# Interleaved runs of columns in the MLP's matmuls: another order for the moving operand and the PSUM output

## The chip, the cores and the metric

The kernel runs on one core of a Trainium2 chip. The metric is the device time of one execution in microseconds (us); smaller is better. The kernel before took 358.94 us (median of 2 runs, 358.88 and 359.0).

## The reference

The program adds three terms: the input `x` (2048 tokens of 448 channels), a gated long convolution of branch A, and an MLP on the layer-normalised input. Cut to what matters:

```python
x = A_q                                    # (1, 2048, 448), float32
xn = _layernorm(x, axis=-1)
# branch A: short causal convolution of k (4 taps), times v, long causal
# convolution with ssm_k through a 4096-point FFT, plus kv * ssm_D, times xn
# branch B:
h = xn @ w1 + b1                           # w1: 448 x 1792
sp = log1p(exp(-|h|)) + max(h, 0)
act = h * tanh(sp)                         # Mish
out = x + A(xn, k, v, ...) + act @ w2      # w2: 1792 x 448
```

The change touches branch B alone. What it computes stays the same.

## The kernel before, in words

**Branch A** is an FFT written as matmuls in plain float32. Its three steps on TensorE are a first transform (`f1_mm`, line 148), an inner transform with its inverse (`f2_mm`, line 237, and `i1_mm`, line 276) and a last transform (`i2_mm`, line 330). They work on parts of the 128 x 128 array: the call at line 237 makes eight matmuls of 448 columns, each on its own block of 64 rows and 32 columns of the array, and the trace holds two records for each of them. VectorE does the four taps, the products and the folds between these steps, GpSimd one tap of each group. Intermediate results go through DRAM.

**Branch B** splits each float32 operand into a high part, rounded to the type `fp32r`, and a low part, and adds three products (high x high, high x low, low x high). The 2048 tokens form 8 chunks of 256 tokens (`CH`), the 1792 inner channels 14 tiles of 128, taken two at a time: a *pair* is one chunk `c` with two inner tiles, `p` from 0 to 6. There are 8 x 7 = 56 pairs, worked in order. For each pair:

- `g1_mm` (line 494) makes 2 x 11 = 22 matmuls at line 514. The stationary operand is a 128 x 128 block of `w1h` or `w1l`, the moving one 256 contiguous columns of `XH` or `XL`, and the output 256 contiguous columns of a PSUM bank. The two inner tiles `n` share a bank, one in each half.
- `mish` (line 517) has ScalarE apply Mish to each 256 columns of PSUM (line 522) into the tile `a`, then cast `a` to its high part `ach` (line 86); VectorE subtracts for the low part `acl` (line 87).
- `g2_mm` (line 536) makes 2 x 2 x 3 = 12 matmuls at lines 546 to 548. The stationary operand is a 128 x 128 block of `ach` or `acl`, the moving one 448 contiguous columns of `w2h` or `w2l`, the output 448 contiguous columns of a PSUM bank, which sums over the seven pairs of the chunk. VectorE then adds that bank to `x` (line 553).

**The order of the work** is written out by hand: a plan by half-slots says when each step of branch A, each load and each split is issued, and `mlp_slot` puts the second layer of a pair two pairs after its first (`G2_LAG`). Each engine takes its instructions in that order. In the octave stage of branch A (slots 66 to 89) the PSUM banks are shared: `mish` of some pairs reads a bank that a transform matmul writes next.

Of the kernel before, what the change touches and what calls it, by code (L numbers as in the profile page):

```python
# [9 lines left out]
AF = mybir.ActivationFunctionType  # L10
# [6 lines left out]
NF = F // 128  # L17
# [21 lines left out]
EVAC_SOON = 2,  # L39
WARM_N = (448, 448, 448)  # L40
FILL_N = (224, 112, 96)


@with_exitstack
def tile_kernel(ctx: ExitStack, tc, q, qT, k, v, sk, hT, sD, w10, w1, w2, c_fib, c_g, c_gi, c_i2, out):
    nc = tc.nc
# [25 lines left out]
    b1t = cp.tile([128, NF], F32, name="b1t")  # L72
# [9 lines left out]
    w2h = wp.tile([128, NF, D], F32R, name="w2h")  # L82
    w2l = wp.tile([128, NF, D], F32R, name="w2l")

    def split(h, l, raw):
        nc.scalar.copy(h, raw)  # L86
        V.tensor_sub(l, raw, h)  # L87
# [4 lines left out]
    def bank(n):  # L92
        return duo[n // 2][:, n % 2]

    def pg():
        return g1p[0].tile([128, 512], F32, name="pg1")
# [9 lines left out]
    def dv(n=1):  # L106
        for _ in range(n):
            if drip:
                drip.pop(0)()
# [257 lines left out]
    def w1_hi(p, a=0, b=256):  # L367
        nc.scalar.copy(w1h[:, :, 256 * p + a:256 * p + b], w1_raw(p, a, b))

    def w1_lo(p, a=0, b=256):  # L370
        fs, rw = slice(256 * p + a, 256 * p + b), w1_raw(p, a, b)
        V.tensor_sub(w1l[:, :, fs], rw[:, 0:3], w1h[:, 0:3, fs])  # L372
        V.tensor_sub(w1h[64:128, 3, fs], rw[64:128, 3], w1h[64:128, 3, fs])
# [120 lines left out]
    def g1_mm(i):  # L494
        c, p = pairs[i]
        XH, XL = XS[c]
        pt = [(bank(GB[i]) if i in GB else pg()).rearrange("p (a b) -> p a b", a=2) for _ in range(2 if i == 0 else 1)]
        ps = [pt[n % len(pt)][:, n] for n in range(2)]
        mm = [[], []]
        for n in range(2):  # L500
            f = 2 * p + n
            fs = slice(128 * f, 128 * f + 128)
            hh, hl, lh = ([(w[:, kt, fs], x[:, kt]) for kt in range(3)] for w, x in ((w1h, XH), (w1h, XL), (w1l, XH)))
            th, tl = ((w1h[:, 3, fs], x[:, 3]) for x in (XH, XL))
            mm[n] = [(n, *m) for m in hh + lh + [th] + hl + [tl]]

            if 0 < i < NP:
                mm[n] = [(n, *m) for m in hh + hl + lh + [th, tl]]
        if i == 0:
            seq = mm[0][:7] + mm[1][:3] + mm[0][7:] + mm[1][7:10] + mm[1][3:7] + mm[1][10:]  # L510
        else:
            seq = mm[0] + mm[1]
        for n_, (n, l, r) in enumerate(seq):
            nc.tensor.matmul(ps[n], l, r, start=all(m[0] != n for m in seq[:n_]), stop=all(m[0] != n for m in seq[n_ + 1:]))  # L514
        P1[i] = ps

    def mish(i):
        p = pairs[i][1]
        ps = P1.pop(i)
        a = mp.tile([128, 2, CH], F32, name="a", bufs=2)  # L520
        for n in range(2):
            nc.scalar.activation(a[:, n], ps[n], AF.Mish, bias=b1t[:, 2 * p + n:2 * p + n + 1])  # L522
            if i == n == 0:
                w1_hi(2)
        if i == 0:
            w1_lo(2)
        ah = mp.tile([128, 2, CH], F32R, name="ach", bufs=3)
        al = mp.tile([128, 2, CH], F32R, name="acl", bufs=3)
        AHL[i] = ah, al
        if 2 * i + 1 in hv:  # L530
            held.append(lambda: split(ah, al, a))
        else:
            split(ah, al, a)
            dv()

    def g2_mm(i, jjs=(0, 1)):
        c, p = pairs[i]
        ah, al = AHL[i]
        for n in range(2):
            f = 2 * p + n  # L540
            for jj in jjs:
                if f == 0:
                    P2[c, jj] = g2p.tile([128, 512], F32, name="pg2")
                ps = P2[c, jj][:, :D]
                cs = slice(128 * jj, 128 * jj + 128)
                nc.tensor.matmul(ps, ah[:, n, cs], w2h[:, f], start=f == 0, stop=False)  # L546
                nc.tensor.matmul(ps, ah[:, n, cs], w2l[:, f], start=False, stop=False)  # L547
                nc.tensor.matmul(ps, al[:, n, cs], w2h[:, f], start=False, stop=f == NF - 1)  # L548

    def g2_evac(c, jjs=(0, 1)):  # L550
        x = Q[c]
# [9 lines left out]
    def mlp_slot(s):  # L561
# [3 lines left out]
        if half == 0:  # L565
            if i < n:
                c, p = pairs[i]
                if c + 1 < NT:
                    if p == 0:
                        ln_load(c + 1)  # L570
                    if p == (3 if c in (0, 2) else 2):
                        ln_stats(c + 1)
                    if c == 0:
                        dv(len(drip))
                    if p == NP - 1:
                        ln_T(c + 1, 1)
                g1_mm(i)
        else:
            if i < n:
                c, p = pairs[i]  # L580
                if p == NP - 2 and c + 1 < NT:
                    ln_T(c + 1, 0)
                if s not in hv:
                    mish(i)
            if 0 <= j < n - 1:
                g2_mm(j)
                if pairs[j][1] == NP - 1 and pairs[j][0] in EVAC_SOON:
                    g2_evac(pairs[j][0])
            elif j == n - 1:
                for jj in range(2):  # L590
                    g2_mm(j, (jj,))
                    g2_evac(pairs[j][0], (jj,))
# [79 lines left out]
    for c in range(NT, NCHUNK):  # L672
        at_ = NT_HOW.get(c, NT_AT)
        b = 2 * NP * (c - 1) + (1 if c < 5 else 0)
# [42 lines left out]
    ps = [g2p.tile([128, 512], F32, name="pg2") for _ in range(2)]  # L717
# [3 lines left out]
    def filler(n, w=wz):  # L721
        k = w.shape[1]
        nc.tensor.matmul(fill[0:k, 0:n], w, wz[:, 0:1].to_broadcast([128, n]), start=True, stop=True)

    filler(FILL_N[0], ve[:, 0:1])
    filler(FILL_N[1], ve[:, 1:2])
    for jj in range(2):
# [3 lines left out]
        if jj == 0:  # L731
            filler(FILL_N[2])
            w1_hi(0, 0, 128)
# [13 lines left out]
    for s in range(nslots):  # L747
        j = s // 2 - G2_LAG - 1
        if s % 2 == 0 and j >= 0 and pairs[j][1] == NP - 1 and pairs[j][0] not in EVAC_SOON:
            g2_evac(pairs[j][0])  # L750
        if s in hv:
            mish(s // 2)
        for fn, args in plan.pop(s, ()):
            fn(*args)
        mlp_slot(s)
        fns = plan2.pop(s, ())
        for fn, args in fns:
            if fn is i1_out:
                fn(*args)
        for fn, args in fns:  # L760
            if fn is not i1_out:
                fn(*args)
# [69 lines left out]
```

## Time and profile before

| what | value |
|---|---|
| median of the runs | 358.94 us (358.88, 359.0) |
| profiled execution: span from first to last instruction | 357.0 us |
| TensorE (PE) busy | 351.0 us, 98% of the span, 3092 matmul records |
| weight loads (PEld) busy | 289.5 us, 81% |
| VectorE (DVE) busy | 270.6 us, 76% |
| ScalarE (ACT) busy | 156.6 us, 44% |
| GpSimd (POOL) busy | 70.3 us, 20% |
| mean granted TensorE clock | 0.998 |

The profile gives for the profiled execution its span alone, not a time of its own measured as the runs are. The median of the runs is 1.9 us above that span; this is what lies around the first and the last instruction.

How to read it: a row of a group names the line, the engine, the operation, output<-inputs, the shapes and the count, then busy us, the mean ns of one instruction and the idle time before them. A matmul's duration covers its way through the array, and the next one starts before it ends. What a matmul costs in a stream is therefore the distance from its start to the next start, which the timeline and the chain of waits show, not its duration. All matmul operands read `f32` there, `fp32r` too.

### The profile page before, as it was taken

The numbers are of one execution on the slowest core, as the hardware profiler recorded it, in microseconds if no ns is written. First come the engines' busy times: TensorE is split into PE (matmuls) and PEld (weight loads), VectorE is DVE, ScalarE is ACT, GpSimd is POOL, SyncE is SP. The second block draws the span as 40 slices with busy tenths as digits, with TensorE's granted clock in tenths as the row PEclk, the third lists the DMA queues.
The fourth block names the chain that finished last, engine by engine and source line by source line (L and its number), as shares of the span: only waits on it lengthen the run. The fifth ranks groups of instructions, "written<-read, shape, count | busy, mean of one in ns | idle before, by whom it ended". The sixth has DMA issues, their size and how long they took to land.

```text
span 357.0 us, 7437 instructions
## 1 busy us (share of the span) xinstructions
PE 351.0 (98%) x3092; PEld 289.5 (81%) x3092; DVE 270.6 (76%) x375; ACT 156.6 (44%) x267; POOL 70.3 (20%) x78
## 2 busy tenths in 40 slices
PE   8999999999999999999999999999999999999995
PEld 2988888888888989888988757666775699979794
DVE  5989748999999999999437756756963933788941
ACT  4966552344243343343233454445445443354470
POOL 2037002822220240212000031011031116040030
PEclk9999999999999999999999999999999999999999
DMA  7998976949768637665869569999896387989086
GB/s 260 344 364 307 411 287 175 340 123 263 198 171 313 164 107 168 223 162 118 245 201 355 201 165 292 248 278 312 276 273 121 77 234 272 409 319 274 19 116 141
DMA packets 30691, 83.27 MB, mean 233 GB/s; under 512 B 3137, under 2 KB 15810, under 8 KB 30658
## 3 DMA queue, kind: packets, MB, share of 16 engines
q1 hardware_dynamic: 21842, 47.82, 39.4%
q0 software_dynamic: 4928, 22.95, 22.9%
q10 hardware_dynamic: 3888, 12.03, 12.8%
q8 instruction: 24, 0.39, 0.4%
q14 instruction: 9, 0.07, 0.1%
HBM read 54.34 MB, written 28.45 MB: 232 GB/s over the span
## 4 chain that ended last, share of the span: by engine, by line
PE 52%; issue 8%; DVE 6%; POOL 2%; DMA 1%
PE pq L514 7%; PE pg L546 7%; PE pg L548 7%; PE pg L547 6%; PE pp L514 5%; PE pr L514 4%; PE pp L237 3%; PE pr L237 3%; PE pp L276 2%; PE pg L514 2%; DVE x L201 2%; POOL x L184 2%; PE pq L237 2%; DMA xn<-in_qT_dram 1%; PE pr L276 1%
## 5 line engine op out<-in xcount | busy, mean ns | idle before, releaser
L546 PE MATMUL pg<-w2h,ach 128*128 128x448 f32 x224 | 82.5, 368 | 0.0
L548 PE MATMUL pg<-w2h,acl 128*128 128x448 f32 x224 | 81.4, 363 | 0.0
L547 PE MATMUL pg<-w2l,ach 128*128 128x448 f32 x224 | 81.2, 362 | 0.0
L87 DVE TENSOR_TENSOR acl<-a,ach 128x512 fp32r<-128x512 f32 x56 | 38.9, 695 | 31.7 <-ACT ach L86 31.5
L522 ACT ACTIVATE a<-pg,b1t 128x256 f32<-128x256 f32 x66 | 27.8, 472 | 65.4 <-PE pg L514 43.3
L514 PE MATMUL pg<-XH,w1h 128*128 128x256 f32 x264 | 52.6, 283 | 0.0
L546 PEld LDWEIGHTS pg<-w2h,ach 128*128 128x128 f32 x224 | 41.9, 187 | 11.5 <-issue 7.2
L514 PEld LDWEIGHTS pg<-XH,w1h 128*128 128x128 f32 x264 | 41.4, 188 | 6.9 <-issue 5.6
L547 PEld LDWEIGHTS pg<-w2l,ach 128*128 128x128 f32 x224 | 42.1, 188 | 2.4
L548 PEld LDWEIGHTS pg<-w2h,acl 128*128 128x128 f32 x224 | 42.1, 188 | 2.4
L514 PE MATMUL pg<-XL,w1h 128*128 128x256 f32 x264 | 42.9, 277 | 0.0
L158 DVE TENSOR_TENSOR st<-pq,st 128x896 f32<-128x896 f32 x32 | 34.8, 1089 | 4.8 <-ACT st L154 4.3
L514 PEld LDWEIGHTS pg<-XL,w1h 128*128 128x128 f32 x264 | 35.9, 188 | 0.0
L86 ACT CAST ach<-a 128x512 fp32r<-128x512 f32 x56 | 34.8, 622 | 1.7
L514 PE MATMUL pg<-XH,w1l 128*128 128x256 f32 x198 | 33.6, 278 | 0.0
L184 POOL TENSOR_TENSOR x<-kr,skb 128x896 f32<-128x896 f32 x8 | 17.0, 2123 | 70.9 <-PE pr L148 26.2
L514 PEld LDWEIGHTS pg<-XH,w1l 128*128 128x128 f32 x198 | 27.6, 188 | 0.2 <-DVE w1l L372 0.2
L201 DVE TENSOR_TENSOR x<-x 128x896 f32<-128x896 f32 x24 | 26.2, 1091 | 1.5 <-POOL x L184 0.8
L522 ACT ACTIVATE a<-pq,b1t 128x256 f32<-128x256 f32 x20 | 8.4, 471 | 31.8 <-PE pq L514 31.8
L287 POOL DMA_DIRECT2D E<-qe x14 | 8.7, 628 | 63.1 <-ACT qe L284 63.1
L154 ACT COPY st<-pr 128x896 f32<-128x896 f32 x16 | 14.5, 908 | 14.2 <-PE pr L148 12.3
L417 POOL TENSOR_TENSOR mv<-ve,mhalf 128x2 f32<-128x2 f32 x5 | 5.0, 1007 | 72.0 <-DVE ve L414 72.0
(138 smaller groups left out, 605.7 us busy)
## 6 DMA issues: line engine op xcount, KB each, us to landing
Dkv<-st ACTq DMA_DIRECT2D x16, 448.0 KB, 5.3
ah<-Dh SPq DMA_DIRECT2D x8, 896.0 KB, 7.5
av<-Dkv SPq DMA_DIRECT2D x8, 896.0 KB, 8.6
e<-E POOLq DMA_DIRECT2D x8, 896.0 KB, 7.2
E<-qe POOLq DMA_DIRECT2D x14, 448.0 KB, 5.9
kr<-in_k_dram SPq DMA_DIRECT2D x10, 448.0 KB, 6.8
Dh<-st ACTq DMA_DIRECT2D x10, 448.0 KB, 6.2
x<-in_hT_dram SPq DMA_DIRECT2D x8, 448.0 KB, 6.0
```

What stands on the lines that cost most here:

```text
L86: nc.scalar.copy(h, raw)
L87: V.tensor_sub(l, raw, h)
L154: nc.scalar.copy(st[:, 1], o)
L158: f(st[:, n], e, st[:, 1])
L184: nc.gpsimd.tensor_mul(o, KR[g - u // 2], skb[:, u:u + 1].to_broadcast([128, 2, D]))
L201: V.tensor_add(KV[g], KV[g], o)
L237: nc.tensor.matmul(p[32 * t:32 * t + 32, r, :D], g[rs, t, c], a[rs, t], start=True, stop=True, tile_position=(64 * r, 32 * t))
L514: nc.tensor.matmul(ps[n], l, r, start=all(m[0] != n for m in seq[:n_]), stop=all(m[0] != n for m in seq[n_ + 1:]))
L522: nc.scalar.activation(a[:, n], ps[n], AF.Mish, bias=b1t[:, 2 * p + n:2 * p + n + 1])
L546: nc.tensor.matmul(ps, ah[:, n, cs], w2h[:, f], start=f == 0, stop=False)
L547: nc.tensor.matmul(ps, ah[:, n, cs], w2l[:, f], start=False, stop=False)
L548: nc.tensor.matmul(ps, al[:, n, cs], w2h[:, f], start=False, stop=f == NF - 1)
```

## The change

Two tables give run lengths for some pair numbers `p`; `p = 0` is in neither and stays as it was. A helper turns 2·b·c contiguous columns into b groups of two runs of c columns: run 0 of the first half, run 0 of the second half, run 1 of the first half, and so on. The columns are the same, in another order.

- **Second layer** (`RUNS`): for p = 1 to 6 the moving operand and the PSUM output are both taken in runs of 16, 8, 32, 2, 4 and 112 columns, the two halves being 224 columns apart. Both are permuted alike, so each column lands where it did before.
- **First layer** (`RUNS1`, run length of the read and of the write; 0 is contiguous; the halves are 128 columns apart): p = 1 reads and writes in runs of 16, p = 5 in runs of 2. There too each column lands where it did. p = 2 reads in runs of 16 and p = 3 in runs of 2, and both write contiguously, so PSUM holds the columns in another order; `mish` restores it by writing `a` in such runs. p = 4 reads contiguously and writes in runs of 16; `mish` reads PSUM in such runs.

Counts, from the loops: 8 chunks x 5 pairs x 22 = 880 of the 1232 first-layer matmuls, 8 x 6 x 12 = 576 of the 672 second-layer matmuls, and 8 x 3 x 2 = 48 of the 112 activations. Every instruction is still one instruction with the same number of columns, and every engine has the same instructions in the same order.

```diff
+RUNS = {1: 16, 2: 8, 3: 32, 4: 2, 5: 4, 6: 112}
+RUNS1 = {1: (16, 16), 2: (16, 0), 3: (2, 0), 4: (0, 16), 5: (2, 2)}
...
+        ri, ro = RUNS1.get(p, (0, 0))
         for n_, (n, l, r) in enumerate(seq):
-            nc.tensor.matmul(ps[n], l, r, start=all(m[0] != n for m in seq[:n_]), stop=all(m[0] != n for m in seq[n_ + 1:]))
+            nc.tensor.matmul(runs(ps[n], ro), l, runs(r, ri), start=all(m[0] != n for m in seq[:n_]), stop=all(m[0] != n for m in seq[n_ + 1:]))
         P1[i] = ps
+
+    def runs(t, c):
+        return t.rearrange("p (a b c) -> p b a c", a=2, c=c) if c else t
 
     def mish(i):
...
-            nc.scalar.activation(a[:, n], ps[n], AF.Mish, bias=b1t[:, 2 * p + n:2 * p + n + 1])
+            ri, ro = RUNS1.get(p, (0, 0))
+            o = runs(a[:, n], ri) if ro != ri else a[:, n]
+            nc.scalar.activation(o, runs(ps[n], ro) if ro != ri else ps[n], AF.Mish, bias=b1t[:, 2 * p + n:2 * p + n + 1])
...
     def g2_mm(i, jjs=(0, 1)):
         c, p = pairs[i]
+        r = (lambda t: t.rearrange("p (a b c) -> p b a c", a=2, c=RUNS[p])) if p in RUNS else lambda t: t
...
-                nc.tensor.matmul(ps, ah[:, n, cs], w2h[:, f], start=f == 0, stop=False)
-                nc.tensor.matmul(ps, ah[:, n, cs], w2l[:, f], start=False, stop=False)
-                nc.tensor.matmul(ps, al[:, n, cs], w2h[:, f], start=False, stop=f == NF - 1)
+                nc.tensor.matmul(r(ps), ah[:, n, cs], r(w2h[:, f]), start=f == 0, stop=False)
+                nc.tensor.matmul(r(ps), ah[:, n, cs], r(w2l[:, f]), start=False, stop=False)
+                nc.tensor.matmul(r(ps), al[:, n, cs], r(w2h[:, f]), start=False, stop=f == NF - 1)
```

## The prediction

> **What bounds the kernel now.** I read the page's totals first, then its chain of work, then the list of what the matmuls waited for, and last the distances between matmul starts. The page:
>
> ```profile
> span 357.0 us, 7437 instructions
> PE 351.0 (98%) x3092; PEld 289.5 (81%) x3092; DVE 270.6 (76%) x375; ACT 156.6 (44%) x267; POOL 70.3 (20%) x78
> ...
> PEclk9999999999999999999999999999999999999999
> ...
> PE 52%; issue 8%; DVE 6%; POOL 2%; DMA 1%
> ```
>
> TensorE is busy from end to end at its full granted clock, and the chain that ended last runs mostly through it. Since a busy PE is not a PE at its peak, the list of waits of the matmul row decides whether there is slack (line, what it waited for, us in total, times, longest):
>
> ```profile
> PE pq L148 <- DVE x L204: 0.7, 1, 0.7
> PE pg L696 <- DVE wz L692: 1.0, 1, 1.0
> PE pg L723 <- DVE ve L414: 0.2, 1, 0.2
> ```
>
> That is all of it: 1.9 us in the whole span, most of it at the start. VectorE is the only other engine near its limit, and only in the stage with branch A's taps. The busy time by stretches of 20 us (the columns are PE, PEld, DVE, ACT, POOL, then clock and DMA) shows the first and the last of five such stretches, and a later one:
>
> ```profile
> 60.00:80.00 20.00, 20.00 (x168) 17.57 (x161) 18.54 (x26) 8.09 (x14) 11.81 (x7) 1.00 0.64 212
> ...
> 140.00:160.00 20.00, 20.00 (x153) 17.58 (x153) 19.56 (x32) 8.60 (x16) 3.16 (x2) 1.00 0.67 200
> ...
> 260.00:280.00 20.00, 20.00 (x255) 12.90 (x261) 10.97 (x12) 7.96 (x12) 3.86 (x6) 1.00 0.72 175
> ```
>
> So TensorE's stream sets the time. Whatever a matmul costs more adds to the span about one for one, since nothing there waits long enough to absorb it. A saving would be kept only where VectorE is not full as well.
>
> The price of a matmul in that stream, first the second layer, from the timeline (start us, duration us):
>
> ```profile
> 240.91 0.36 PE L546 MATMUL pg<-w2h,ach 128*128 128x448 f32 x1
> 241.11 0.36 PE L547 MATMUL pg<-w2l,ach 128*128 128x448 f32 x1
> 241.31 0.36 PE L548 MATMUL pg<-w2h,acl 128*128 128x448 f32 x1
> ...
> 243.11 0.37 PE L548 MATMUL pg<-w2h,acl 128*128 128x448 f32 x1
> ```
>
> The first and the twelfth matmul of this pair start 2.20 us apart, so eleven steps of 0.200 us: 0.446 ns a column. For the first layer, the chain of waits in order of time (start us, us, what):
>
> ```profile
> 171.90 2.51 PE pg L514 x22
> 174.40 0.20 PE pg L546
> ...
> 176.80 2.51 PE pg L514 x22
> ```
>
> 22 matmuls of 256 columns take 2.51 us: 0.114 us each, again 0.446 ns a column. A pair takes 176.80 - 171.90 = 4.90 us.
>
> **The change part by part.** The sum is made against the profiled execution: span 357.0 us, and 1.9 us around it to the median of 358.94.
>
> *The matmuls.* 576 x 0.200 = 115.2 us of the second layer and 880 x 0.114 = 100.3 us of the first get another order of columns, 215.5 us or 60% of the span. Nothing is added or moved: weight loads, semaphores, number of columns and order stay. The one question is whether a stream in runs goes at 0.446 ns a column too. No matmul of the trace reads or writes in runs, so I bound it from the nearest rows.
>
> The free end is the row that I have, contiguous columns: no change. [...]
>
> ```profile
> 235.92 0.96 PE L237 MATMUL pq<-ah,g 64*32 64x448 f32 x16
> ...
> 236.67 0.96 PE L237 MATMUL pr<-av,g 64*32 64x448 f32 x16
> ...
> 237.42 0.96 PE L237 MATMUL pp<-av,g 64*32 64x448 f32 x16
> ```
>
> Sixteen records in 0.75 us are two on each of eight blocks of the array: 0.375 us for 448 columns, or 0.1875 us at half that. If the 0.200 hides a stall of reading or writing that another order avoids, 576 x (0.200 - 0.1875) = 7.2 us and 880 x (0.114 - 0.107) = 6.2 us could be gained: -13.4 us.
>
> The dear end is the same record taken as a price: a stream that gets a column only every other step pays 0.375 instead of 0.200 us for 448 columns, +0.175 us, and by the same ratio +0.100 us for 256. On all changed matmuls that would be 576 x 0.175 + 880 x 0.100 = +188.8 us.
>
> Between these ends I look at what runs cost other engines in this trace:
>
> ```profile
> L86 ACT CAST ach<-a 128x512 fp32r<-128x512 f32 x56 | 34.8, 622 | 1.7
> ...
> L460 ACT CAST XH<-xn 128x512 fp32r<-128x512 f32 x10 | 6.2, 624 | 13.7 <-DVE xn L453 13.7
> ```
>
> ```profile
> L453 DVE TENSOR_TENSOR xn<-xn,con 128x512 f32<-128x512 f32 x20 | 13.8, 689 | 1.4 <-DMA con<-MR 1.0
> ...
> L461 DVE TENSOR_TENSOR XL<-xn,XH 128x512 fp32r<-128x512 f32 x10 | 6.9, 689 | 3.2 <-ACT XH L460 3.1
> ```
>
> Line 86 reads and writes 512 contiguous columns, line 460 four runs of 128: 622 against 624 ns. Line 453 reads every second element of a row, line 461 does not: 689 ns both. Address patterns are free there, but at more than 1 ns a column; TensorE asks for one every 0.446 ns, so this speaks for the free end without proving it. I take no change for the matmuls, being nearest to these rows, and keep the dear prices as rivals.
>
> [...]
>
> *The activations.* 48 of them read PSUM or write SBUF in runs of 16 or 2.
>
> ```profile
> L522 ACT ACTIVATE a<-pg,b1t 128x256 f32<-128x256 f32 x66 | 27.8, 472 | 65.4 <-PE pg L514 43.3 <-DMA Dkv<-st 14.6 <-DMA Dh<-st 3.4
> ```
>
> At the price of the two casts above it is nothing; at a doubling, 48 x 0.47 = 22.6 us on ScalarE. That engine is 44% busy and waits 43.3 us at this line for the matmuls. The consumer, the pair's second layer, comes two pairs or some 9.8 us later. Queued behind the activation are the cast of line 86 and the copies that free PSUM for branch A. Where TensorE was held up by an activation, the weight loads show it:
>
> ```profile
> PEld pg L546 <- ACT a L522: 1.4, 2, 0.7
> ...
> PEld pp L237 <- ACT a L522: 0.9, 4, 0.2
> ```
>
> 2.3 us in six waits. The four at line 237 are where `mish` frees a bank for a transform (slots 69, 75, 81, 87: pairs 34, 37, 40, 43, with p = 6, 2, 5, 1); of these only p = 2 gets a changed activation. Even doubled, that is 0.94 us at one place. I take 0, and up to 2 us for the range.
>
> *Sum:* 357.0 + 0 + 1.9, that is 358.9 us.
>
> **The rivals.**
>
> *B, runs of two at half rate.* A fetch that brings more than two neighbouring columns, or a PSUM access that wants its neighbours next, is used for two columns only, and the stream falls to every other step; from runs of four on it is hidden. This decides at p = 4 of the second layer (96 matmuls) and p = 3 and 5 of the first (352): 96 x 0.175 + 352 x 0.100 = 52.0 us, 411 us. If only the write suffers, p = 3 falls out: 16.8 + 17.6 = 34.4 us, 393 us. For it speaks that the contiguous stream is already above 0.1875 us, as if near a limit of its supply; against it, the free step of two on VectorE.
>
> *C, any write to PSUM in runs at half rate.* All 576 of the second layer and p = 1, 4, 5 of the first (528): 100.8 + 52.8 = 153.6 us, 512 us. Nothing in this trace speaks for so much; nothing excludes it either, since every matmul before writes contiguously. [...]
>
> *D, a lost column at each jump.* Each run begins with an address that does not follow on. At one column, 0.446 ns, and 438 runs over the six second-layer forms x 96 plus 304 over the five first-layer forms x 176 = 95,552 runs: 42.6 us, 401 us; at half a column 380 us. The long runs (112, 32) would hardly show it.
>
> *E, faster.* The -13.4 us above, less the 100 of 357 us (60 to 160) in which VectorE is about full: some 9.6 us, 349 us. It needs the new order to cure the 0.0125 us by which a matmul is above branch A's record, and I see no reason for that.
>
> That the change does nothing, because a pattern is folded back to plain columns, would give the forecast's time.
>
> **How the numbers follow.** Forecast A (no change) 0.54; B 0.20; C 0.12; D 0.11; E 0.03. A's own range is 357.5 to 363: no change within the runs' spread, the 2 us of activations and a small cost of the long runs. 2% is 7.2 us, about what a measurement here can tell from no change; a slowing of the changed stream by 3.3% reaches it. Faster therefore has 0.03, within 2% 0.54, slower 0.43. The range goes from 357 to 412: it holds A, D and B, 0.85, and leaves out C and E.
>
> **What would show it.** In the profile after, start-to-start distances by form: 0.200 us and 0.114 us in every pair for A; 0.375 and 0.214 in the pairs with runs of two for B, with durations near 536 ns as at line 237; the same in every pair with a PSUM write in runs for C; distances growing with the number of runs (2 against 112) for D. The activations of p = 2, 3, 4 would show their own price against 472 ns, and the weight loads whether anyone waited for it. The forecast is wrong if a second-layer form (96 matmuls) is over 0.075 us dearer, or a first-layer form (176) over 0.041: each alone makes 7.2 us.

## The result and the profile after

The changed kernel takes 390.97 us (median, 390.8 to 391.13) against 358.94 us: 1.089 times as long, 95% interval 1.0871 to 1.0909. That is slower by 32.0 us, inside the predicted range of 357 to 412, but the point forecast of 358.9 us (no change) was wrong.

The page of the changed kernel, with totals and the chain of work:

```profile
span 389.3 us, 7440 instructions
PE 384.4 (99%) x3092; PEld 310.3 (80%) x3092; DVE 271.7 (70%) x375; ACT 156.9 (40%) x267; POOL 69.5 (18%) x78
...
PE 99%; DVE 0%; issue 0%
```

TensorE's busy time grew by 33.4 us and the span by 32.3; VectorE, ScalarE and GpSimd did the same work in the same time, to about 1 us, and a weight load of the second layer took 189 ns against 188 before. The chain, which ran through VectorE and "issue" in places before, now runs through TensorE alone, and the matmul row waits for one thing only, at the start:

```profile
PE pg L705 <- DVE wz L701: 1.0, 1, 1.0
```

So the 32 us lie in the matmul stream itself. The chain of waits in order of time (start us, us, what; line 517 is the first layer, 555 to 557 the second) shows in which pairs, here of chunk 2:

```profile
97.43 2.64 PE pg L517 x22
...
109.66 3.83 PE pg L517 x22
...
116.02 2.50 PE pg L517 x22
...
121.05 3.67 PE pg L517 x22
...
128.34 2.50 PE pg L517 x22
...
131.43 0.29 PE pg L557
```

These are p = 1 (reads and writes in runs of 16), p = 3 (reads in runs of 2), p = 4 (writes in runs of 16), p = 5 (reads and writes in runs of 2), p = 6 (unchanged) and a second-layer matmul of p = 4 (runs of 2). The writes of p = 4 cost nothing (2.50 us for the 22, as in the unchanged p = 6), and p = 5, which also writes in runs, is no dearer than p = 3, which does not (3.67 against 3.83 us). The median distance from one matmul's start to the next, taken from all start times of the two traces by pair number, gives the whole account:

| form (read, write) | count | before, us | after, us | sum, us |
|---|---|---|---|---|
| first layer p = 1 (16, 16) | 176 | 0.114 | 0.120 | 1.1 |
| p = 2 (16, contiguous) | 176 | 0.113 | 0.120 | 1.2 |
| p = 3 (2, contiguous) | 176 | 0.113 | 0.164 | 9.0 |
| p = 4 (contiguous, 16) | 176 | 0.113 | 0.113 | 0 |
| p = 5 (2, 2) | 176 | 0.1135 | 0.166 | 9.2 |
| second layer p = 4 (2) | 96 | 0.201 | 0.287 | 8.3 |
| p = 5, 1, 2, 3, 6 (4, 16, 8, 32, 112) | 480 | 0.201 | 0.213, 0.211, 0.210, 0.2095, 0.206 | 4.3 |

Together 33.1 us, against 32.3 in the span. Reads in runs of two make 26.5 us of it, longer runs 6.6. The activations, which write or read in runs too, stayed near their price of 472 ns:

```profile
L530 ACT ACTIVATE a<-pg,b1t 128x256 f32<-128x256 f32 x66 | 28.0, 475 | 85.1 <-PE pg L517 73.6 <-DMA Dkv<-st 4.5 <-DMA Dh<-st 3.6
```

By pair number, those of p = 2 and 4 took 471 and 474 ns on average, and only those of p = 3, which write SBUF in runs of two, took more: 489 instead of 471 ns, 0.3 us for all sixteen. No matmul waited for one.

### The profile page after: what moved, and what is told of

The parts are those of the page before. It is cut to its first block, busy times and chain, and to the rows that moved or that the text cites. A ratio compares the mean times of both kernels' runs of the same rounds, so it can differ in the third digit from the quotient of the medians.

```text
span 389.3 us, 7440 instructions
## 1 busy us (share of the span) xinstructions
PE 384.4 (99%) x3092; PEld 310.3 (80%) x3092; DVE 271.7 (70%) x375; ACT 156.9 (40%) x267; POOL 69.5 (18%) x78
## 4 chain that ended last, share of the span: by engine, by line
PE 99%; DVE 0%; issue 0%
PE pg L517 25%; PE pg L555 13%; PE pg L557 13%; PE pg L556 13%; PE pq L517 8%; PE pp L517 5%; PE pr L517 5%; PE pq L150 4%; PE pr L239 2%; PE pp L239 2%; PE pp L278 2%; PE pq L239 2%; PE pr L278 1%; PE pg L705 1%; PE pp L332 1%; PE pg L468 1%
## 5 line engine op out<-in xcount | busy, mean ns | idle before, releaser
L555 PE MATMUL pg<-w2h,ach 128*128 128x448 f32 x224 | 87.5, 390 | 0.0
L557 PE MATMUL pg<-w2h,acl 128*128 128x448 f32 x224 | 85.8, 383 | 0.0
L556 PE MATMUL pg<-w2l,ach 128*128 128x448 f32 x224 | 85.8, 383 | 0.0
L517 PE MATMUL pg<-XH,w1h 128*128 128x256 f32 x264 | 56.8, 299 | 0.0
L517 PEld LDWEIGHTS pg<-XH,w1h 128*128 128x128 f32 x264 | 43.2, 190 | 7.7 <-issue 5.6
L517 PE MATMUL pg<-XL,w1h 128*128 128x256 f32 x264 | 47.1, 294 | 0.0
L517 PEld LDWEIGHTS pg<-XL,w1h 128*128 128x128 f32 x264 | 38.9, 190 | 0.0
L517 PE MATMUL pg<-XH,w1l 128*128 128x256 f32 x198 | 36.7, 295 | 0.0
L517 PEld LDWEIGHTS pg<-XH,w1l 128*128 128x128 f32 x198 | 29.8, 190 | 0.1
L203 DVE TENSOR_TENSOR x<-x 128x896 f32<-128x896 f32 x24 | 26.5, 1104 | 1.1 <-POOL x L186 0.2
```

Of the source, the lines that this page charges most:

```text
L203: V.tensor_add(KV[g], KV[g], o)
L517: nc.tensor.matmul(runs(ps[n], ro), l, runs(r, ri), start=all(m[0] != n for m in seq[:n_]), stop=all(m[0] != n for m in seq[n_ + 1:]))
L555: nc.tensor.matmul(r(ps), ah[:, n, cs], r(w2h[:, f]), start=f == 0, stop=False)
L556: nc.tensor.matmul(r(ps), ah[:, n, cs], r(w2l[:, f]), start=False, stop=False)
L557: nc.tensor.matmul(r(ps), al[:, n, cs], r(w2h[:, f]), start=False, stop=f == NF - 1)
```

## The experiments

Where a fence shows windows (start:end, length, busy PE, granted clock, DMA share, GB/s), the step is the window's length divided by the matmuls that start in it (12 or 10); the count in a row is higher where matmuls that began earlier still run.

**The change without its runs of two.**

```diff
-RUNS = {1: 16, 2: 8, 3: 32, 4: 2, 5: 4, 6: 112}
-RUNS1 = {1: (16, 16), 2: (16, 0), 3: (2, 0), 4: (0, 16), 5: (2, 2)}
+RUNS = {1: 16, 2: 8, 3: 32, 5: 4, 6: 112}
+RUNS1 = {1: (16, 16), 2: (16, 0), 4: (0, 16)}
```

> The changed kernel without its runs of two: p = 4 of the second layer and p = 3 and 5 of the first are contiguous again, all longer runs stay. Theory 1 (the cost lies in reading the moving operand in runs of two): the forms left cost 0.005 to 0.013 us a matmul in the changed kernel's trace, 576 - 96 of the second layer and 352 first-layer reads in runs of 16, together some 6.7 us above the kernel before: about 365.6 us, and 25 to 27 us of the 32 are gone. Rival (a cost of any run, which shows most where runs are many): the second layer's runs of 4 and 8 keep the total above 375 us.

Measured: 365.18 us, 1.0171 times the kernel before (1.0154 to 1.0188). Its page:

```profile
span 363.4 us, 7438 instructions
## 1 busy us (share of the span) xinstructions
PE 358.2 (99%) x3092; PEld 292.6 (81%) x3092; DVE 271.0 (75%) x375; ACT 156.9 (43%) x267; POOL 70.3 (19%) x78
```

25.8 of the 32.0 us are gone, as theory 1 had it to half a microsecond. Most of the 6.2 us left belongs to the longer runs, whose steps are those of the table above within 1 ns. But the median step also rose at p = 3 and 4 of the first layer, which read contiguously there: 0.117 and 0.118 us against 0.113, at most 1.6 us in all.

**Writes alone, all of them in runs of two.** Every MLP matmul reads contiguously and writes PSUM in runs of two; the readers of PSUM follow.

```diff
+RUNS = {}
+RUNS1 = {p: (0, 2) for p in range(7)}
...
+        o = lambda t: runs(t, 2)
...
-                nc.tensor.matmul(r(ps), ah[:, n, cs], r(w2h[:, f]), start=f == 0, stop=False)
...
+                nc.tensor.matmul(o(ps), ah[:, n, cs], w2h[:, f], start=f == 0, stop=False)
...
-            V.tensor_add(x[:, jj], P2.pop((c, jj))[:, :D], x[:, jj])
+            y = x[:, jj].rearrange("p (b a c) -> p b a c", a=2, c=2)
+            V.tensor_add(y, runs(P2.pop((c, jj))[:, :D], 2), y)
```

> All 1904 matmuls of the MLP read contiguously, as in the kernel before, and write PSUM in runs of two; the activations and VectorE's additions read PSUM in such runs. Theory 1 (reads alone cost): steps stay at 0.200 and 0.114 us and the total at 359 us, plus or minus 2. Rival (a PSUM write in runs costs a stall too, which the read of the same matmul hid in the changed kernel): the second layer's step goes to 0.287 and the first's to 0.166, which is 672 x 0.087 + 1232 x 0.052 = 122 us more, 481 us.

Measured: 359.1 us, 1.0001 times the kernel before (0.9992 to 1.0011). The group of one second-layer line, before (line 546) and in this run, and VectorE's addition:

```profile
L546 PE MATMUL pg<-w2h,ach 128*128 128x448 f32 x224 | 82.5, 368 | 0.0
```

```profile
L558 PE MATMUL pg<-w2h,ach 128*128 128x448 f32 x224 | 82.5, 368 | 0.0
```

```profile
L566 DVE TENSOR_TENSOR qt<-pg,qt 128x448 f32<-128x448 f32 x16 | 9.3, 616 | 4.1 <-PE pg L560 4.1
```

368 ns, as before; 616 ns, against 617 at line 553. The steps are unchanged too, 0.201 us in the second layer and 0.113 to 0.114 us in the first, at every pair number. A PSUM write in runs of two cost nothing in these streams, in 1904 matmuls, nor did VectorE's reads of it (616 ns) or ScalarE's (472 ns at line 533, as at line 522 before).

**Other steps between the runs.** Does the cost come from the distance of the two halves? A pair (a, c) cuts the operand into a parts and takes a run of c from each in turn.

```diff
+RUNS = {1: (112, 2), 2: (56, 2), 3: (28, 2), 4: (14, 2), 5: (7, 2), 6: (4, 2)}
+RUNS1 = {1: (0, 2), 2: (0, 4), 3: ((64, 2), 0), 4: ((16, 2), 0), 5: ((4, 2), 0), 6: (4, 0)}
```

> Runs of two columns everywhere in the second layer but p = 0, with steps of 4, 8, 16, 32, 64 and 112 columns between one run and the next (p = 1 to 6) instead of a jump of 224; the write follows the read. First layer: p = 1 writes in runs of 2, p = 2 in runs of 4; p = 3, 4, 5 read in runs of 2 with steps of 4, 16 and 64 columns; p = 6 reads in runs of 4. Theory 1 (each visit to an aligned group of four columns takes a least time, 0.287 us / 224 = 1.28 ns, and a run of two uses half of it): all six second-layer forms at 0.287, the three reads of the first layer at 0.166, the writes at 0.114, runs of 4 at 0.12; total about 359 + 576 x 0.087 + 528 x 0.052 = 437 us. Theory 2 (a cost of the jump, whatever its size): the same here. Theory 3 (the two halves, 224 or 128 columns apart, fall on the same part of the memory and collide): the forms differ, and the small steps, which walk on through the operand, cost little or nothing.

Measured: 532.54 us, far above all three theories. The windows of one pair for p = 1, 2, 3, 4, 5 and 6, in this order (start:end, length, busy PE):

```profile
149.91:154.67 4.76, 4.76 (x13) 1.00 0.97 299
36.29:41.22 4.93, 4.93 (x20) 1.00 0.91 374
228.98:233.53 4.55, 4.55 (x13) 1.00 0.50 99
117.23:121.90 4.67, 4.67 (x14) 1.00 0.82 204
62.76:67.94 5.18, 5.18 (x15) 1.00 0.01 3
253.36:258.07 4.71, 4.71 (x20) 1.00 0.00 0
```

Twelve matmuls each: 0.397, 0.411, 0.379, 0.389, 0.432 and 0.393 us, where the form with the jump of 224 had taken 0.287 (the medians of the distances are 0.397, 0.404, 0.378, 0.384, 0.413 and 0.387). The first layer's reads in runs of 2, with steps of 4, 16 and 64 (p = 3, 4, 5), took 0.229, 0.220 and 0.227 us, all double the contiguous step of 0.113; its writes in runs of 2 and 4 took 0.114 and 0.117, its reads in runs of 4 0.126. Theory 3 falls: a small step costs as much as a large one. So do theory 2, since no form kept the 0.287, and the time of 1.28 ns in theory 1. A run of two that walks on through the operand takes 0.397 us / 224 = 1.77 ns. That is just what four contiguous columns take, 0.200 us / 112 = 1.79 ns. What is paid for seems to be the group of four, not the column; and the two halves of the changed kernel come back to a group after one other visit, at which the second visit seems to be cheap: 0.287 us / 112 = 2.56 ns for two visits, 1.77 + 0.79. This is a reading so far; the kernels below test it.

**Runs that start in the middle of a group.** The second layer's weights are moved by two columns. Two small tiles change as well: `rstd` is shortened and `ve1` shares the tile `one`; no MLP matmul reads them.

```diff
-    w2h = wp.tile([128, NF, D], F32R, name="w2h")
-    w2l = wp.tile([128, NF, D], F32R, name="w2l")
+    w2h, w2l = (wp.tile([128, NF * D + 2], F32R, name=n)[:, 2:].rearrange("p (f d) -> p f d", f=NF) for n in ("w2h", "w2l"))
...
+RUNS = {1: 4, 2: 8, 3: 16, 4: 2, 5: 32, 6: 112}
+RUNS1 = {1: (64, 0), 2: (32, 0), 3: (8, 0), 4: (4, 0), 5: ((32, 4), 0), 6: ((8, 4), 0)}
```

> The second layer's weights lie two columns (8 bytes) later in memory, so a run of 4, 8, 16, 2, 32 or 112 columns (p = 1 to 6) starts in the middle of an aligned group of four; p = 0 is contiguous and shifted. The first layer only sweeps aligned reads: runs of 64, 32, 8, 4 (p = 1 to 4), and runs of 4 with steps of 8 and 32 columns (p = 5, 6). Theory 1 (time per visit to an aligned group of four): a run of 4 is now two half groups and costs as runs of 2 do, 0.287; a run of 8 takes 1.28 + 1.79 + 1.28 ns, 0.244 us; a run of 16 0.222; 32 about 0.213; 112 and the runs of 2 as before, 0.206 and 0.287; p = 0 stays at 0.200. Theory 2 (length of the run, wherever it starts): as in the changed kernel, 0.213, 0.210, 0.211, 0.287, 0.207, 0.206. The first layer's sweep shows whether the small cost of long runs (0.006 us at runs of 16) grows with the number of runs or is one price per matmul; by theory 1 all lie between 0.114 and 0.122.

Measured: 403.83 us. The windows of one pair for p = 0, 1, 2, 3, 4, 5, 6 (contiguous, runs of 4, 8, 16, 2, 32, 112):

```profile
109.28:111.82 2.54, 2.54 (x14) 1.00 0.57 191
115.57:119.06 3.49, 3.49 (x14) 1.00 1.03 229
270.47:274.25 3.78, 3.78 (x14) 1.00 0.82 301
171.71:174.75 3.04, 3.04 (x14) 1.00 0.30 53
134.96:138.51 3.55, 3.55 (x14) 1.00 0.78 204
141.15:144.03 2.88, 2.88 (x14) 1.00 0.04 8
102.98:105.62 2.64, 2.64 (x14) 1.00 0.40 131
```

Per matmul 0.212, 0.291, 0.315, 0.253, 0.296, 0.240 and 0.220 us (the medians of the distances are up to 9 ns lower). Theory 2 falls: runs of 4 that cost 0.213 aligned cost 0.291 when each spans two half groups. In these two forms the place of a run in memory decided, not its length. Theory 1's numbers for runs of 8 (0.244) and 16 (0.222) were too low; if every group visited costs 1.76 ns (0.394 us / 224, as the next kernel gives it), 3 groups a run of 8 make 56 x 3 x 1.76 = 0.296 us, and 28 x 5 x 1.76 = 0.246 for runs of 16. For runs of 4 the same count gives 112 x 2 x 1.76 = 0.394, which is too much. These come back to a half-used group after two other visits, the runs of 8 only after three; with a cheap second visit (0.83 ns, an estimate: two columns at half the float32 record's 0.375 us / 448), 113 x 1.76 + 111 x 0.83 makes 0.291. These sums are estimates made after the result. The aligned sweep of the first layer stayed small: median distances of 0.120, 0.119, 0.122, 0.127, 0.118 and 0.120 us for p = 1 to 6 (only the 0.127 of the runs of 4 lies above the 0.122 expected), with 0.120 at the unchanged p = 0 of this kernel, whose tiles lie elsewhere.

**Other types.** Groups of ten matmuls of 448 columns are added behind the last output.

```diff
+    for n, cs in (("tb", (0, 16, 8, 4, 2, (112, 2), (56, 4), (28, 8))), ("tr", (0, 16, 8, 4, 2, (112, 2))), ("tf", (0, 16, 4, 2, (112, 2)))):
+        t = tiles[n]
...
+                nc.tensor.matmul(tp_[:, :D], t[:, :128], runs(t[:, :], c), start=True, stop=True)
```

> The MLP as before the change, no runs anywhere; behind the last output stand added groups of ten matmuls of 448 columns on a constant operand in bf16, fp32r and float32, contiguous and in runs of 16, 8, 4 and 2 (two halves 224 columns apart), and in runs that use half of what they pass over (2 of 4, 4 of 8, 8 of 16 columns). Nothing of the output changes. Theory 1 (a least time of some 1.28 ns for each visit to an aligned 16 bytes, here eight bf16 columns or four of the others): bf16 contiguous at 0.19 us, runs of 8 and of 4 free, runs of 2 about 0.28; fp32r as in the kernel, 0.20 contiguous, 0.287 at runs of 2; float32, which takes four times as long a column, shows no cost at runs of 2. Theory 1b (the share of the fetched bytes that is used decides): bf16 runs of 4, half of 16 bytes, cost as fp32r runs of 2 do, some 0.28, and runs of 2 more, 0.5. Theory 2 (a stall at the jump): float32 at runs of 2 has the same +0.087 us a record.

The windows of one group each: bf16 with runs of 16, 8, 4 and 2, with a step of 4 (112, 2) and of 8 (56, 4); fp32r with runs of 4 and 2 and (112, 2); float32 (two records a matmul) contiguous, with runs of 2 and (112, 2):

```profile
363.25:365.14 1.89, 1.89 (x11) 1.00 0.05 9
365.14:367.03 1.89, 1.89 (x11) 1.00 0.00 0
367.03:369.00 1.97, 1.97 (x11) 1.00 0.00 0
369.00:371.37 2.37, 2.37 (x11) 1.00 0.00 0
371.37:373.34 1.97, 1.97 (x11) 1.00 0.00 0
373.34:375.31 1.97, 1.97 (x11) 1.00 0.00 0
...
383.53:385.66 2.13, 2.13 (x11) 1.00 0.00 0
385.66:388.55 2.89, 2.89 (x11) 1.00 0.00 0
388.55:392.50 3.95, 3.95 (x11) 1.00 0.02 4
...
396.27:400.03 3.76, 3.76 (x11) 1.00 0.00 0
...
415.06:419.00 3.94, 3.94 (x11) 1.00 0.00 0
...
422.93:426.87 3.94, 3.94 (x11) 1.00 0.00 0
```

bf16 is barely touched: 0.189 us down to runs of 8, 0.197 at runs of 4 and 0.237 at runs of 2, where theory 1 said 0.28 and theory 1b more. But the bf16 numbers fit 1.76 ns a group of 16 bytes, which holds eight bf16 columns: (112, 2) and (56, 4) visit 112 such groups in the 0.197 us measured, and contiguous reading only 56, by this estimate 56 x 1.76 = 0.099 us, well under the 0.189 us that the stream took (0.422 ns a column). Runs of 2 from the two halves fit with cheap returns to a group: 56 x (1.76 + 3 x 0.83) = 0.238, against 0.237 measured. float32, whose records take 0.376 us for 448 columns, pays 0.394 = 224 x 1.76 with the step of 4: no stall of 0.087 (theory 2), but not free either, as theory 1 had it. It takes the same 0.394 with runs of 2 from two halves, where half of the visits are returns. Contiguous fp32r took 0.207 us here (median) and not 0.201 as in the kernel; why is open. Two fp32r columns of each group visited gave half speed here (0.395 us), four just about full speed (0.213).

**Is contiguous reading itself held back by the fetch?** Theory 4 puts this together and says so; if it is right, fp32r columns that are read twice must go faster than contiguous ones.

```diff
+    def twice(t, c):
+        return t[:, :192].rearrange("p (g o c) -> p g o c", o=1, c=c).to_broadcast([128, 192 // c, 2, c])
...
+        forms = [t, twice(t, 4), twice(t, 8), runs(t, (96, 2))] + [runs(t, (a, c)) for c in (2, 4) for a in (2, 3, 4, 6)]
...
+                nc.tensor.matmul(tp_[:, :384], tiles["w" + n], m, start=True, stop=True)
```

> The MLP as before the change; behind the last output stand added groups of twelve matmuls of 384 columns (the weights in a tile of their own, operands constant), in bf16 and in fp32r: contiguous; each group of four or of eight columns read twice in a row; runs of 2 with a step of 4; runs of 2 and of 4 columns taken in turn from 2, 3, 4 and 6 equal parts of the operand. Nothing of the output changes. Theory 4, formed from the last five kernels: the read has to fetch aligned 16 bytes (four fp32r or eight bf16 columns) at 1.76 ns each, also where it is contiguous; a fetched group is held while a few others are visited, and then gives its other columns at the stream's own 0.417 ns. fp32r: contiguous 96 x 1.76 = 0.169 us plus a few ns; four or eight columns twice 0.163, the stream's own rate; step of 4 192 x 1.76 = 0.338; runs of 2 from two parts 96 x (1.76 + 0.83) = 0.249, from three parts the same if three groups are held, from four and six parts 0.338; runs of 4 at 0.169 from any number of parts. bf16: contiguous 0.163; runs of 2 from two parts 48 x (1.76 + 3 x 0.83) = 0.204, from four and six parts 0.338; runs of 4 from two parts 0.165, from four and six 0.169. Rival (theory 5: contiguous fp32r is not held back by fetches but by a rate of its own, 0.446 ns a column): reading four columns twice stays at 0.171 us.

The windows of twelve matmuls each, first bf16 with runs of 2 from 2, 3 and 4 parts; then fp32r contiguous, four columns twice, eight columns twice, step of 4, and runs of 2 from 2, 3, 4 and 6 parts:

```profile
369.16:371.60 2.44, 2.44 (x13) 1.00 0.00 0
371.60:374.26 2.66, 2.66 (x13) 1.00 0.00 0
374.26:378.17 3.91, 3.91 (x13) 1.00 0.00 0
...
389.97:392.19 2.22, 2.22 (x14) 1.00 0.00 0
392.19:394.14 1.95, 1.95 (x13) 1.00 0.00 0
394.14:396.30 2.16, 2.16 (x14) 1.00 0.00 0
396.30:400.37 4.07, 4.07 (x13) 1.00 0.00 0
400.37:403.35 2.98, 2.98 (x13) 1.00 0.00 0
403.35:406.73 3.38, 3.38 (x13) 1.00 0.00 0
406.73:410.76 4.03, 4.03 (x13) 1.00 0.00 0
410.76:414.77 4.01, 4.01 (x13) 1.00 0.00 0
```

The contiguous fp32r group begins with one matmul that waits; its median distance is 0.173 us. Four columns twice take 1.95 / 12 = 0.1625 us, the rate of contiguous bf16 (0.163), with half the groups to visit. Theory 5 (0.171) falls. Runs of 2 take 0.248 us from two parts (0.249 expected), 0.282 from three, 0.336 and 0.334 from four and six (0.338), and 0.339 at the step of 4; bf16 0.203, 0.222 and 0.326 (0.204, none given for three, 0.338). Read by theory 4, these times say that a fetched group is still there after one other visit, partly after two and no longer after three. (The shifted runs of 4, at 0.291, behaved as if it were fully there after two; that difference is open.) Two numbers were missed: eight columns twice at 0.180 instead of 0.163, and fp32r runs of 4 from 2, 3, 4 and 6 parts at 0.194, 0.193, 0.177 and 0.208 (medians) instead of 0.169.

**What the longer runs cost.** These misses, 8 to 39 ns a matmul, are of the size of the 5 to 12 ns by which the longer runs of the changed kernel are dearer, or larger. Two parts are read in turn, 192 to 320 columns apart.

```diff
+    def two(d, c):
+        v = t[:, :2 * d].rearrange("p (a x) -> p a x", a=2)[:, :, :192]
+        return v.rearrange("p a (b c) -> p b a c", c=c) if c else v
...
+    forms = [(d, c) for c in (4, 16, 64) for d in (192, 196, 200, 208, 224, 256, 320)] + [(192, 0), (224, 0), (256, 0)]
```

> The MLP as before the change; behind the last output stand added groups of twelve fp32r matmuls of 384 columns on a constant operand, which read two parts of 192 columns in turn, in runs of 4, 16 and 64, with the parts 192, 196, 200, 208, 224, 256 and 320 columns apart, and the two parts one after the other. Nothing of the output changes. By theory 4 every form visits 96 groups of four once, 0.169 us plus a few ns, as contiguous reading (0.173 us); yet runs of 4 took 0.177 to 0.208 us in the last kernel. Theory 6 (the rest is a collision of the two parts, set by how far apart they are): the time changes with the distance, alike for runs of 4, 16 and 64 or weaker with longer runs. Theory 7 (a fixed cost of some ns for each jump): 96 jumps cost most, 24 a quarter, 6 almost nothing, at any distance.

Windows of twelve: runs of 4 at distances of 208 and 256, runs of 16 at 208 and 256, runs of 64 at 208, and the parts one after the other:

```profile
370.55:372.71 2.16, 2.16 (x13) 1.00 0.00 0
...
374.91:377.20 2.29, 2.29 (x13) 1.00 0.00 0
...
386.00:388.16 2.16, 2.16 (x13) 1.00 0.00 0
...
390.33:392.49 2.16, 2.16 (x13) 1.00 0.00 0
...
401.01:403.09 2.08, 2.08 (x13) 1.00 0.00 0
...
409.40:411.48 2.08, 2.08 (x13) 1.00 0.03 8
```

Neither theory holds alone. Runs of 4 move with the distance, from 0.180 us at 208 columns to 0.191 at 192, 256 and 320; runs of 16 stay at 0.180 to 0.182 at any distance, and runs of 64 at 0.173 to 0.178. The number of jumps matters but not in proportion: 24 jumps cost 7 ns, 96 at the best distance no more. What this small cost is stays open; it makes some 6 of the 32 us. A contiguous fp32r stream has a spread of the same size (0.113 to 0.120 us in the first layer, 0.201 to 0.207 for 448 columns), so it need not be a cost of runs alone.

This trace shows one thing more. In the first group (40 matmuls in 9.11 us, at a mean granted clock of 0.81) the granted clock was 0.50 for a while (358.14 to 360.70 us), and there the runs of 4, at a distance of 192, took 0.320 us each, just as contiguous bf16 did at that clock in the kernel before this one (40 in 8.17 us, mean 0.79). At full clock they took 0.191 against 0.1625. So the time of the runs of 4 did not double with the halved clock, which would have made 0.382 us.

## Why the prediction was wrong, point by point

- **What bounds the kernel** was right: the whole cost of the matmuls reached the span (33 us of stream, 32 us of span), and nothing absorbed it.
- **The forecast A** failed at one step, "I take no change for the matmuls, being nearest to these rows". The rows were VectorE's and ScalarE's, which took 1.35 and 1.21 ns a column (689 and 622 ns for 512). Line 453, one operand of which uses two columns of each 16 bytes, takes 1.35 ns a column and so reaches the next 16 bytes every 2.7 ns, more slowly than the 1.76 ns a group on TensorE: at such a price it would not have shown the cost. TensorE took a bf16 column every 0.42 ns (0.189 us / 448); at that rate four fp32r columns, a whole group, go in 1.69 ns, less than the 1.76. The prediction stated that difference of rate and then set it aside. Both signs of being wrong that it named came: 0.086 us at p = 4 of the second layer, 0.051 and 0.052 at p = 3 and 5 of the first.
- **The range** held the result only because it had been stretched over rivals B and D; forecast A's own range ended at 363.
- **Rival B** (0.20) was the right mechanism at the right place, with the runs of two alone, but on the read side only, and mis-sized: +0.086 and +0.052 us instead of +0.175 and +0.100, so 26.5 us and not 52.0. The price had been taken from the float32 record, whose 0.375 us is not what its groups cost: contiguous float32 took 0.376 us for 112 groups (estimate 112 x 1.76 = 0.197), and 0.394 for 224. By luck it is near the price of a run of two that does not come back to its group: 0.397 instead of 0.200 with the step of 4.
- **The sign for it was in the profile.** Contiguous fp32r took 0.446 ns a column where half of the float32 record gave 0.1875 us / 448 = 0.4185 ns; that the array does step so fast was the author's assumption then, which bf16 later bore out (0.189 us). The prediction read the gap as "near a limit of its supply" and gave it little weight. With groups of four columns it gives a price for every form: 1.79 ns for a new group, 0.84 for two columns of a held one, so 112 x 2.63 = 0.294 us and 64 x 2.63 = 0.168, which is 96 x 0.094 + 352 x 0.054 = 28 us. Two things the trace could not show: that the supply comes in groups of four fp32r columns, which the later kernels bear out, and that a group is held between two visits; without the second the price would have been near B's (224 x 1.79 = 0.401 us against 0.375).
- **Rival C** (0.12) is refuted here for runs of two: 1.0001 with all 1904 writes in such runs. Its half rate for any write in runs was an assumption that no run shows; the writes in runs of 16 left the first layer's step at 0.113 us.
- **Rival D** (0.11), a lost column of 0.446 ns at each jump, would have cost 112 x 0.446 = 0.050 us at the second layer's runs of 4; they cost 0.012. Its time of 401 us came near by luck.
- **Rival E** asked whether the contiguous stream hides a stall of reading: by this account it does, 0.173 against 0.1625 us for 384 columns. Then no order of the same columns avoids it, since every group has to be fetched once; none that was tried was faster than contiguous.
- **The activations** at nothing: right to 0.3 us of ScalarE's time.

## What to carry to other kernels

Compare a stream's step with what the array itself can do (here fp32r's 0.201 us with bf16's 0.189); where it is longer, ask whether its supply is the limit: here reads that used two columns of each group visited took 0.287 us and, with no return to the group, 0.378 to 0.413, instead of 0.201. For fp32r operands keep the moving operand's runs in whole, aligned groups of 16 bytes (runs of 4 took 0.213 us aligned and 0.291 shifted by two columns), while the PSUM output may be scattered in runs of two at no measured cost (1.0001). Do not carry over a price of address patterns from a slower engine (VectorE's row, at 1.35 ns a column, showed none).

## What the runs showed of the hardware

- Reads of the moving operand with no return to a group took about 1.76 ns for each group of 16 bytes visited, in the three types: 0.395 us for 224 groups of fp32r, 0.394 for 224 of float32, 0.197 for 112 of bf16. Over the six steps of the second layer it was 1.69 to 1.84 ns.
- Contiguous fp32r took 0.173 us for 384 columns against 0.1625 when each group is read twice; contiguous bf16 took 0.163.
- fp32r runs of two in turn from two parts, which come back to a group after one other visit, took 0.248 us for 384 columns; from three parts, after two visits, 0.282; from four parts, after three, 0.336, against 0.339 with no return.
- At a granted clock of 0.50 fp32r runs of 4 took 0.320 us, as contiguous bf16 did; at full clock 0.191 against 0.1625.
- PSUM writes in runs of two columns left the steps of 1904 matmuls as they were, 0.201 us in the second layer and 0.113 to 0.114 in the first.
